# LayerNorm sums from Gram blocks on TensorE, and a parameter stage in one searched order, in a four-layer kernel

## The chip, the cores and the metric

One core of one Trainium2 chip. The metric is the device time of one execution in microseconds (us). Single runs of one kernel here spread by about 0.5% (528 us before: 526.3 to 528.9, with one run at 530.7), so several runs are taken, and each kernel is set against the kernel before on the same chip. The experiments came in three batches, the first and third on one chip and the second on another. Kernels of different batches are therefore compared by their ratios to the kernel before; 11 of the third batch's 12 runs of before are those of the first. Engines: PE (TensorE), DVE (VectorE), ACT (ScalarE), POOL (GpSimd), SP (sync, which issues most transfers). "PEld" in the profile is PE's weight load. The "granted clock" is the PE clock that the chip allowed in a stretch, as a share of full speed (1.00). Every run told of here was classed as fast, not disturbed.

## The reference

Input x is 2048 x 512 in bf16. Four layers, each added to x after a LayerNorm: convolution, attention, convolution, attention. Both convolutions have the same parameters.

```python
def conv(u, A_re, A_im, B_re, B_im, C_re, C_im, log_dt, Dskip):   # u: LayerNorm(x)
    dt = exp(log_dt)[:, None]                     # 512 channels
    P = exp((dt * A)[:, :, None] * l)             # 512 x 128 modes x 2048 steps, l = 0..2047
    K = einsum("dn,dnl,dn->dl", C, P, dt * B).real
    return irfft(rfft(u padded) * rfft(K padded))[:2048] + u * Dskip
def attend(x):                                    # 32 heads of 16, window of 8 at distance 2
    ...                                           # cut
x = x + conv(layernorm(x)); x = x + attend(layernorm(x))
x = x + conv(layernorm(x)); x = x + attend(layernorm(x))
```

## The kernel before

The first stage makes from the parameters the powers of each mode: a *ladder* of ten squarings (lambda, lambda^2, lambda^4, ...), whose values are cast to bf16 *multipliers*. From these DVE builds, for each of eight groups of 64 channels, a *table*: levels 0 to 3 and "high" double the filled part each time (two products and a sum per level), then three products with larger powers. TensorE contracts the table to the convolution kernel. In the same stage the first LayerNorm takes its mean and variance with one DVE statistic instruction per 512 elements of a token, 16 in all.

```python
def ladder(nc, pp, pst, identf, raw, M, cb, fill):
    ...                                             # exp, sin, cos; turned to modes by TensorE
    for i in range(11):
        if i < 10:
            nc.scalar.activation(sq[:], cur[:], ACT.Square)
            nc.vector.scalar_tensor_tensor(nxt[:, 1, :], cur[:, 0, :], 2.0, cur[:, 1, :], ALU.mult, ALU.mult)
            nc.vector.tensor_tensor(nxt[:, 0, :], sq[:, 0, :], sq[:, 1, :], ALU.subtract)
        multipliers(i, cur)                         # up to 4 casts f32 -> bf16, all on ACT
        ...                                         # coefficients at i = 0, the 48th power at i = 5
        fill(i)

def fill(i):
    if 1 <= i <= 4:
        ln.gather(X, 0, (i - 1) * 4, i * 4)         # bn_stats, four at a time
    if i == 4:
        ln.finish(0, NJ)                            # 16 bn_aggr, sqrt, reciprocal, offset
    if i == 10:
        for j in range(NJ):                         # 16 normalisations, all on ACT
            nc.scalar.activation(X[:, j, :], X[:, j, :], ACT.Identity, bias=ln.nb[:, j:j + 1], scale=ln.rstd[:, j:j + 1])
```

The rest of the kernel (first convolution, attention, second convolution, attention) is written as four *plans*: a list of operations with what each must wait for, some of them with alternatives (`either`: on ACT or on DVE, by transfer or by TensorE), and a list of numbers, found by a search, that says in which order they are issued and which alternative is taken.

```python
def run(self):
    order = [int(i) for i in ORDERS[Plan.turn].split()]
    ...
    for i in order:
        fn, after, way = self.ops[i]
        assert done.issuperset(after)
        fn(); done.add(i)
```

## Time and profile before

| | before |
|---|---|
| time, median (3 runs) | 528.13 us (527.34 to 528.93) |
| span of the profile | 525.1 us |
| DVE / PE / ACT busy | 91% / 78% / 65% |
| first stage, 20 to 62 us | DVE and ACT full, PE nearly idle |
| DVE from 62 to 180 us | 116.1 of 118 us busy |

The busy share alone says that DVE is the engine to relieve; the stretches, which the prediction shows below, say where: with DVE full and later stages that wait for it, a microsecond saved early can travel far. It is not certain that it does, because between 20 and 62 us ACT is full as well.

### The profile page before, as it was taken

Reading aid. Unit: us, or ns where it says so; the run is one execution under the profiler, and the core shown is the slowest. Engines: PE = TensorE matmul, PEld = TensorE weight load, DVE = VectorE, ACT = ScalarE, POOL = GpSimd, SP = SyncE. Lnnn points to the kernel's source line nnn. Section 1 sums busy time; section 2 is a strip of 40 time slices with the busy share of each in tenths; the row PEclk is TensorE's granted clock in tenths of the full one; section 3 lists DMA queues with packets and bytes.
Section 4 is the critical chain, followed back from the end, with each engine's and each line's share of the span. In section 5 each row is a group of like instructions: output and inputs, shape, how many; then the busy total and the mean of one; then the engine's idle time right before and its main releaser. Section 6 shows DMA issues by size and latency. Waiting matters only on the chain.

```text
span 525.1 us, 11929 instructions
## 1 busy us (share of the span) xinstructions
PE 407.9 (78%) x4973; PEld 239.1 (46%) x4973; DVE 475.4 (91%) x803; ACT 339.2 (65%) x505; POOL 12.9 (2%) x62
## 2 busy tenths in 40 slices
PE   0201367788869769899999788969997999998896
PEld 0100245456646647543456234555774334653342
DVE  4999999999999999759899998889989597999995
ACT  3999966886866768772766137989996436641230
POOL 0000000000000003100000000000000000000000
PEclk9999997989998999999999999999999999998998
DMA  8300073149125253460011422679401600222252
GB/s 264 156 1 0 0 142 92 46 131 163 43 104 122 48 157 108 138 121 31 0 62 49 103 40 41 182 214 167 82 2 20 101 31 31 71 56 55 41 134 88
DMA packets 88923, 45.10 MB, mean 86 GB/s; under 512 B 74923, under 2 KB 81068, under 8 KB 88612
## 3 DMA queue, kind: packets, MB, share of 16 engines
q1 hardware_dynamic: 87284, 43.93, 34.3%
q8 instruction: 39, 0.64, 0.5%
q10 hardware_dynamic: 1584, 0.39, 0.4%
q14 instruction: 16, 0.13, 0.1%
HBM read 15.77 MB, written 8.13 MB: 46 GB/s over the span
## 4 chain that ended last, share of the span: by engine, by line
DVE 34%; PE 32%; ACT 10%; issue 9%; DMA 4%; SPq 0%; POOL 0%; DVEq 0%; ACTq 0%
PE ps_qk L1193 10%; DVE prod L1356 7%; PE ps_v L1213 4%; PE Lp L1254 3%; DVE Y2tab L545 3%; DVE Ttab L545 3%; DVE Ttab L488 3%; DVE Ttab L481 3%; DVE Ttab L480 3%; DVE ln_st_b L150 3%; PE ps_o L1429 2%; PE po L1372 2%; PE po L1377 1%; ACT X L598 1%; DVE Ttab L497 1%
## 5 line engine op out<-in xcount | busy, mean ns | idle before, releaser
L1244 DVE TENSOR_TENSOR prod<-qT,kT 128x2048 bf16<-128x2048 bf16 (+1 forms) x80 | 77.2, 1007 | 12.3 <-ACT kT L1198 11.7
L1356 DVE TENSOR_TENSOR prod<-VX,L 128x2048 bf16<-128x2048 bf16 (+2 forms) x96 | 77.6, 868 | 1.7 <-PE po L1377 0.9
L1193 PE MATMUL ps_qk<-xnT,wqk 128*128 128x512 bf16 x256 | 62.3, 381 | 0.6 <-DMA xnT<-xn 0.4
L1372 PE MATMUL po<-prod,sb_ident 128*128 128x512 bf16 x224 | 56.1, 388 | 6.9 <-DVE prod L1356 4.5
L1372 PEld LDWEIGHTS <-sb_ident 128*128 128x128 bf16 x224 | 21.8, 99 | 35.4 <-issue 12.0
L1193 PEld LDWEIGHTS <-wqk 128*128 128x128 bf16 x256 | 22.1, 98 | 31.5 <-issue 10.4
L1213 PE MATMUL ps_v<-wv,xnT 128*128 128x256 bf16 x256 | 32.9, 273 | 1.4 <-ACT xnT L1171 1.2
L1392 ACT CAST ot<-po 128x1024 bf16<-128x1024 f32 x14 | 13.6, 1014 | 29.7 <-PE po L1372 29.7
L1254 PE MATMUL Lp<-prod,sb_bones 128*32 128x512 bf16 x256 | 28.7, 388 | 4.2 <-DVE prod L1244 4.2
L520 PE MATMUL ps_sum<-Ttab,sb_ident 128*128 128x512 bf16 x18 | 7.7, 426 | 30.6 <-DVE Ttab L480 27.6
L716 ACT CAST Z<-ps_s 128x1024 bf16<-128x1024 f32 (+1 forms) x32 | 29.5, 996 | 0.2
L558 PE MATMUL psk<-Ttab 128*32 128x64 bf16 x1024 | 21.7, 204 | 9.6 <-DVE Ttab L545 6.0
L1218 ACT CAST VX<-ps_v 128x512 bf16<-128x512 f32 x32 | 18.8, 587 | 15.6 <-PE ps_v L1213 15.6
L545 DVE TENSOR_TENSOR Ttab<-Ttab,MPA 128x2048 bf16<-128x2048 bf16 (+2 forms) x20 | 28.5, 1436 | 0.3
L561 PE MATMUL psk<-Y2tab,Ttab 128*32 128x48 bf16 x1024 | 21.6, 199 | 8.4 <-issue 7.6
L1429 PE MATMUL ps_o<-wo_t,oT 128*128 128x512 bf16 x112 | 28.0, 379 | 0.0
L1213 PEld LDWEIGHTS <-xnT 128*128 128x128 bf16 x256 | 23.2, 98 | 9.6 <-issue 4.6
L545 DVE TENSOR_TENSOR Y2tab<-Ttab,MPB 128x6144 bf16<-128x6144 bf16 (+1 forms) x13 | 27.2, 2123 | 0.0
L1198 ACT CAST qT<-ps_qk 128x512 bf16<-128x512 f32 x24 | 14.0, 584 | 19.1 <-PE ps_qk L1193 19.1
L150 DVE BATCH_NORM_STATS2 ln_st_b<-X 128x6 f32<-128x128 bf16 (+2 forms) x80 | 22.9, 356 | 3.7 <-ACT X L856 3.3
L1198 ACT CAST kT<-ps_qk 128x512 bf16<-128x512 f32 x26 | 15.2, 584 | 15.9 <-PE ps_qk L1193 15.9
L558 PEld LDWEIGHTS <-Ttab 128*32 128x32 bf16 x1024 | 19.6, 102 | 11.9 <-issue 11.1
(220 smaller groups left out, 1030.6 us busy)
## 6 DMA issues: line engine op xcount, KB each, us to landing
X<-in_A_u_dram SPq DMA_DIRECT2D x8, 512.0 KB, 5.4
kt_scratch<-sp_k SPq DMA_DIRECT2D x16, 256.0 KB, 2.8
Kt<-kt_scratch SPq DMA_DIRECT2D x16, 256.0 KB, 5.9
out_dram<-X SPq DMA_DIRECT2D x4, 512.0 KB, 2.7
k_scratch<-KTq SPq DMA_DIRECT2D x7, 256.0 KB, 2.6
KT<-k_scratch SPq DMA_DIRECT2D x7, 256.0 KB, 2.8
VX<-VX SPq DMA_DIRECT2D x4, 448.0 KB, 3.7
kT<-kT SPq DMA_DIRECT2D x8, 192.0 KB, 2.2
```

Of the source, the lines that this page charges most:

```text
L150: self.nc.vector.bn_stats(self.st[:, j, part, :], X[:, j, a:b])
L545: nc.vector.tensor_tensor(d, src.to_broadcast([128, c, n, 2 * EYB]), mm.to_broadcast([128, c * n, EYB, 2]), ALU.mult)
L558: nc.tensor.matmul(o.rearrange("e (s i) -> e s i", s=2), xs, T[:, 1:3, h, m // 2, :, t], start=(m == 0), stop=False, skip_group_check=True)
L716: nc.scalar.copy(box["Z", kind, dc][:, 0:n // 8, :, jq * 32:(jq + 1) * 32].rearrange("p g r k -> p r g k"), box.pop(("s1", kind, dc, jq))[ ...
L1193: nc.tensor.matmul(ps[:], wqk[:, ct, f0:f0 + 128], xnT[:, 4 * s:4 * s + 4, ct, :], start=(ct == 0), stop=(ct == 3))
L1198: copy((qT, kT)[which][fp][:, f2, o:o + 512], box.pop(("qk", which, fp, f2, s))[:])
L1213: nc.tensor.matmul(ps[:, jj].rearrange("p t h d -> p (t h d)"), xnT[:, j + jj, ct, :], wv[:, ct, fp * 256:(fp + 1) * 256], start=(ct == 0) ...
L1244: nc.vector.tensor_tensor(pr[:, 0:n2], qT[fp][:, a:a + n2, j0 * 128:j0 * 128 + 1024], kT[fp][:, a:a + n2, c0:c0 + 1024], ALU.mult)
L1254: nc.tensor.matmul(Lp[r0:r0 + 32, w // 4, :], bones[:, w % 4, :], pr[:, f2 - a, hb * 512:(hb + 1) * 512], start=(n == 1), stop=(n == 4), s ...
L1356: nc.vector.tensor_tensor(p2[:, 0:nj].rearrange("p j t d h -> p (j t) d h"), VX[:, fp, NV + a:NV + a + nj].rearrange("p j (t d h) -> p (j ...
L1372: nc.tensor.matmul(po[:, c:c + 512], ident[:], p2[:, k + j:k + j + 2].rearrange("p j t d h -> p (j t d h)"), start=(n == 1), stop=(n == W))
L1429: nc.tensor.matmul(ps, box["oT"][:, ft // 2, j, ft % 2, :], wo_t[:, ft, :], start=(ft == 0 and not res), stop=(ft == 3))
```

## The change

The intent: take the LayerNorm sums away from DVE, which is full, and give them to PE, which is idle. X is turned by eight DMA transposes. The 32 x 32 Gram blocks of 32 tokens with themselves have the sums of squares on their diagonals; a product with ones gives the sums. DVE then only masks the diagonals and reduces, once for all 2048 tokens. Second, the whole first stage becomes a fifth plan with a searched order and alternatives of its own (casts and normalisations on ACT or DVE), and the first table and the first levels of the second move into it. Third, the parameters are loaded in runs of 1 KB per partition instead of 256 B. All five orders were searched anew, those of the unaltered later layers too.

```diff
-        eng.dma_start(t[:], prm[name].rearrange("(t p) n -> p t n", p=128))
+        eng.dma_start(t[:], prm[name].rearrange("(p t) n -> p t n", p=128))
...
+def prepare(nc, pp, pst, raw, identf, block, ones, M, cb, T, ln, X):
+    pl = Plan(ptq=2, sq=2, lad=3)
...
+        B = pl.either(("mb", i), lambda: [act(a_sign(0)), act(a_sign(1))], lambda: follow(act(a_sign(0)), opposite()),
+                      lambda: follow(ve(v_sign(0)), opposite()))
...
+        def turn(j2=j2):
+            nc.sync.dma_start(xT[:, j2 * 2:j2 * 2 + 2].rearrange("c j t p -> c (j t) p"),
+                              X[:, j2 * 2:j2 * 2 + 2].rearrange("p j c -> p (j c)"), transpose=True)
+        def mm(j2=j2):
+            for j in (j2 * 2, j2 * 2 + 1):
+                for ct in range(4):
+                    nc.tensor.matmul(rows[:, j:j + 1], xT[:, j, ct, :], ones[:, 0:1], start=(ct == 0), stop=(ct == 3), ...)
+                for ct in range(4):
+                    for g in range(4):
+                        x = xT[:, j, ct, g * 32:g * 32 + 32]
+                        nc.tensor.matmul(gram[g * 32:g * 32 + 32, j, :], x, x, start=(ct == 0), stop=(ct == 3), ...)
+    o = vec(0.61, lambda: nc.vector.tensor_tensor(own[:], gram[:], block[:].unsqueeze(1).to_broadcast([128, NJ, 32]), ALU.mult), gs)
+    o = vec(0.61, lambda: nc.vector.tensor_reduce(sq[:], own[:], axis=AX.X, op=ALU.add), o)
...
+    for lev in range(4):                             # first table, half by half
+        for x in (1, 0):
+            a = vec(2 * us, lambda lev=lev, x=x: T.level(0, lev, x, x + 1), o[x], casts[lev if x else lev + 6])
+            o[x] = vec(us, lambda lev=lev, x=x: T.level_sum(0, lev, x, x + 1), a)
...
+    pl.run()
```

## The prediction

> **What bounds the kernel now.** I read the busy shares in 40 slices first, then the busy time by stretches, then the groups of instructions and the order of time in the first 67 us.
>
> The page's slices (one digit is 13.1 us, in tenths of busy time):
>
> ```profile
> PE   0201367788869769899999788969997999998896
> DVE  4999999999999999759899998889989597999995
> ACT  3999966886866768772766137989996436641230
> ```
>
> DVE (VectorE) is at nine tenths from slice 2 to slice 16, so from 13 to about 205 us; that is the stage which the change rewrites (parameters, first LayerNorm, kernel tables, first convolution). ACT is full only in slices 2 to 5, and PE is nearly empty there. The busy time by stretches (stretch, length, then each engine's busy us with its count) says it in numbers:
>
> ```profile
> 9.00:20.00 11.00, 3.52 (x13) 2.38 (x14) 10.97 (x19) 6.30 (x11) 0.00 (x0) 1.00 0.85 339
> 20.00:31.00 11.00, 0.89 (x4) 0.49 (x3) 11.00 (x19) 11.00 (x20) 0.00 (x0) 1.00 0.00 1
> 31.00:42.00 11.00, 0.00 (x0) 0.00 (x0) 11.00 (x38) 10.97 (x19) 0.00 (x0) 1.00 0.00 1
> 42.00:52.00 10.00, 2.15 (x6) 0.73 (x7) 9.86 (x18) 10.00 (x18) 0.00 (x0) 1.00 0.00 0
> 52.00:62.00 10.00, 2.78 (x16) 1.47 (x15) 9.90 (x8) 10.00 (x15) 0.00 (x0) 1.00 0.00 0
> 62.00:70.00 8.00, 5.61 (x261) 4.87 (x260) 7.13 (x6) 6.64 (x9) 0.00 (x0) 1.00 0.49 82
> ```
>
> From 20 to 62 us DVE and ACT (third and fourth busy figure) are both full and PE is idle. From 62 to 180 us DVE is busy 116.13 of 118 us. So a microsecond of DVE work taken out before 62 us, or of DVE idleness filled, should move everything up to about 205 us forward, provided ACT does not hold it back. The groups of the first 64 us show the work in question (busy us, mean ns):
>
> ```profile
> L150 DVE BATCH_NORM_STATS2 ln_st_a<-X 128x6 f32<-128x512 bf16 x16 | 10.3, 683 | 1.9 <-DMA X<-in_A_u_dram 1.9
> L421 DVE TENSOR_TENSOR lad<-sq 128x512 f32<-128x512 f32 x10 | 6.9, 687 | 0.0
> L159 DVE BATCH_NORM_AGGREGATE ln_mv_a<-ln_st_a 128x2 f32<-128x6 f32 x16 | 1.2, 153 | 0.0
> L598 ACT ACTIVATE X<-X,ln_nb_a,ln_rstd_a 128x512 bf16<-128x512 bf16 x16 | 11.4, 799 | 0.0
> L418 ACT ACTIVATE sq<-lad 128x1024 f32<-128x1024 f32 x9 | 9.4, 1047 | 0.0
> ```
>
> And the order of time shows three places where order, not work, costs:
>
> ```profile
> 9.03 1.88 DVE L150 BATCH_NORM_STATS2 ln_st_a<-X 128x6 f32<-128x512 bf16 x3 [1.89 <-DMA X<-in_A_u_dram]
> 10.83 0.67 DVE L367 TENSOR_TENSOR cs<-sh 128x512 f32<-128x512 f32 x1
> ...
> 15.58 1.06 ACT L418 ACTIVATE sq<-LAM 128x1024 f32<-128x1024 f32 x1
> ...
> 50.95 11.37 ACT L598 ACTIVATE X<-X,ln_nb_a,ln_rstd_a 128x512 bf16<-128x512 bf16 x16
> ...
> 64.38 1.23 DVE L480 TENSOR_TENSOR Ttab<-Ttab,MUA 128x2048 bf16<-128x2048 bf16 x1 [0.80 <-ACT Ttab L525]
> ```
>
> DVE stands 1.89 us for the first rows of X although other work is there; three statistics then delay the cosine, so the ladder of squarings starts only at 15.58; and the second table's level 3 waits 0.80 us for a copy on ACT which stood behind the 16 normalisations. My reference point is the end of that pair of level 3 products of the second table: 66.7 us (the next DVE instruction starts at 66.77).
>
> Overlap matters in the counting: a 128x512 f32 tensor operation lasts 0.69 us, but starts follow at 0.60. I count starts: 0.60 per 512 f32, 0.29, 0.33, 0.60, 1.14, 2.2, 3.27 for bf16 products of 256, 512, 1024, 2048, 4096, 6144; 0.60 per 512-element statistic; on ACT 0.52 per cast, 0.95 per square, 0.71 per normalisation.
>
> **What the Trainium skill says.** "VectorE: DVE Perf Modes", perf-mode tier table: a tensor_tensor in f32, and tensor_reduce in any type, have only the 1x mode; bf16 tensor_tensor 2x; tensor_scalar and copy up to 4x. The trace agrees where it has the case: 687 ns for 512 f32 elements and 684 for 1024 bf16. So the new product with the block mask and the reduction should each cost the 0.60 of an f32 operation. "ScalarE: Activation LUTs", what ACT_TABLE_LOAD costs: about 1283 ns; the trace has three of 1.28 here, and the change needs the same three functions. "TensorE: Matmul & The Clock Gate", back-to-back issue gap: about 25 ns is the floor for up to 64 columns. The trace is faster where four column groups alternate: the table contraction of before issues about 120 such small matmuls per us (15 pairs of four and four in 1.0 us). The 256 Gram matmuls (32x32 outputs in four column groups) are then some 2 to 6 us of an idle PE. "DMA: Bandwidth & Descriptors", DMA Transpose (X-bar): 2-byte types into SBUF, which this is; before's 32 such transposes land a median of 3.5 us after issue and cost about 1.3 us of issue each.
>
> **The change, part by part (DVE before the reference point).** Before: 4.38 to 66.74 is 62.4 us, with idle 0.64 (parameter load), 1.89 and 0.80; so 59.0 us of work.
> - Removed: 16 statistics x 0.60 = 9.6 and 16 aggregations, 1.1: -10.7.
> - Added for the statistics: mask product 0.61, reduction 0.61, three 16-wide operations of about 0.12: +1.6.
> - The first table is now built half by half (levels 0 to 3, twice the instructions at half the size): six operations of about 0.25 / 0.29 / 0.33 / 0.60 instead of three of 0.29 / 0.33 / 0.60 / 1.14: +0.6 +0.75 +0.2 +0.2 = +1.75.
> - Choices that I read by counting the operations in the order in which the new plan makes them and looking up which numbers its order holds: eight multiplier casts go from ACT to DVE (one full cast 0.6, seven half-size bf16 copies at 0.33), +2.9; three of 16 normalisations at 0.32, +1.0; one evacuation of the turned parameters, +0.6; the second table's level 2 sum on DVE instead of PE and ACT, +0.6.
> Sum: -10.7 + 8.4 = -2.3, so 56.7 us of DVE work. The large statistic saving is thus mostly spent on relieving ACT.
>
> ACT, same way: from the start of the ladder it had 62.3 - 15.6 = 46.7 us without a gap. New: 10 squares 9.5, 38 casts (46 before) 19.8, two coefficient copies 1.0, table load with root 1.6, 13 normalisations 9.2: 41.1 us, starting when the ladder can start. With the statistics out of the way and the parameters contiguous (1 KB runs instead of 256 B), I put that at about 13 us, so ACT ends near 54 to 56, and DVE still has the 2.2 + 3.3 us of products after ACT's last multiplier. DVE stays the bound: start near 4.1, 56.7 of work, 0.5 to 2 of idleness for loads and the start of the ladder: 61.3 to 62.8, say 62.0. Gain at the reference point: 4.7 us.
>
> After it, the convolution's own choices, counted the same way: DVE loses two joins and two level sums, gains two other sums and three evacuations: +1.0 us by the durations of those shapes; ACT and PE lose three PE-made turns of spectra (2.8 and 1.4 us), which become DMA. As DVE is 98% busy there, I give back 1.0 of the gain and take 0.3 for less waiting. The convolution should end about 4.0 us earlier. The two attention layers and the second convolution keep their operations; about a dozen choices move (in the first attention layer two residual additions go from DVE to PE and ACT, -0.9 us of DVE; in the last, two evacuations). I credit the new orders with 1.0 us in all. That is my judgement, not a count. Sum: 528.1 - 4.0 - 1.0 = 523.1.
>
> **Rivals.** (a) The statistics fully pay: all 9.1 us (10.7 less 1.6) come through because ACT is what really paces 20 to 62 us, and the moves to DVE fill holes. For it: ACT has no gap there. Against: DVE has none either, and 8 of those 9 us are visibly spent on it. It would give 517 to 519. (b) The turned copy of X comes late and takes the place of the statistics: the eight transposes wait for X on the sync queue and for each other. X landed from 9 us; eight times 1.3 from about 11 plus 3.5 ends near 25; the mask product stands in DVE's order after about 26 us of work, near 30. Margin 4 us; if it fails, DVE or the normalisations wait and the time is 525 to 528. The 2 MB of transform constants are now issued after these transposes, near 23 us, and needed only near 50. (c) What is gained early is lost at the convolution's end: after 207 us before, DVE waits for PE and ACT (1.03 and 1.93 us in single waits), a chain of transfers, turns and copies. If that chain sets the end, only half arrives: about 526. Against: its start hangs on the last table, which DVE makes.
>
> **Range.** The count of DVE work is good to about 1.5 us, its idleness to 1, the later orders to 2. Together about 3: 519.5 to 526.3. Faster by over 2% needs below 517.8, which only rival (a) reaches: 0.07. Slower by over 2%: 0.01.
>
> **What would show it.** Right: none of the 16 first statistics; the mask product and reduction at about 0.69 us with no wait before them; the first square near 13 us; DVE busy about 57 us before the second table's level 3 products end, and that end near 62; normalisations over by 54; the first contraction about 4 us earlier than 65.3; the stretch from there to the last layers unchanged in length to 1 us. Wrong: a DVE wait for PE's Gram sums, half-size copies of multipliers that cost 0.6 instead of 0.33 (then 2 us less gain), or a gain after 205 us larger than before it.

## The result

The changed kernel takes 519.89 us (median of 4 runs, 519.01 to 520.22), before in the same rounds 527.74 (527.29 to 528.93). The ratio is 0.9845, 95% interval 0.9824 to 0.9867. A ratio is formed from the fast runs of both kernels and is near the ratio of their means (here 519.75 over 527.92), not quite that of the medians; for the experiments it is given as recorded, and the listed runs give it again to about 0.001. The saving is 7.85 us; the prediction said 523.1, a saving of 5.0, with 519.5 as the low end of its range. So it holds, but near its edge.

Where the time went, from the two profiles (us from the start; the profiled runs differ by 6.7 us):

| point | before | changed | shift |
|---|---|---|---|
| DVE through with the work of the first stage (first table, second table to the level 3 products) | 66.7 | 60.4 | -6.3 |
| first contraction on PE | 65.3 | 61.5 | -3.9 |
| last table products start on DVE | 193.6 | 187.7 | -5.9 |
| last X of the first convolution arrives (statistics start) | 219.5 | 216.4 | -3.2 |
| first projection of the first attention | 228.3 | 225.0 | -3.3 |
| first matmul of the second convolution | 344.1 | 340.8 | -3.3 |
| last matmul of the second convolution | 396.9 | 392.1 | -4.8 |
| end | 525.1 | 518.4 | -6.7 |

Three things stand in this table: a gain of 6.3 us in the first stage, a loss of 2.7 between 188 and 220 us, and another 3.4 us gained after 340 us, where the operations are the same but for a few choices of engine. (The medians differ by 7.85 us, the two profiled runs by 6.7; the table cannot place the other 1.1.)

A caution: the granted clock and small waits move such points. The changed kernel, profiled again with the experiments, had a span of 520.3. A single profile's points are good to 1 or 2 us, stage lengths in undisturbed stretches to some tenths.

The page of the changed kernel, busy tenths in 40 slices (13.0 us each):

```profile
PE   1600768688869887899999879979997999997896
DVE  6999999999999998768899998799899498999995
ACT  4999877569658756653655437989996447632330
```

PE now has six tenths of work in slice 2 (mostly the Gram blocks), where it had two; the first runs of full slices end one slice earlier, for DVE after slice 15 instead of 16 and for ACT after slice 4 instead of 5. The stretches of the same time as shown of before (stretch, length, then busy us and count of PE, PEld, DVE, ACT, POOL, then clock, DMA share and GB/s):

```profile
9.00:20.00 11.00, 6.96 (x136) 5.24 (x136) 10.31 (x23) 6.08 (x10) 0.00 (x0) 1.00 0.80 199
20.00:31.00 11.00, 4.47 (x200) 3.75 (x200) 10.66 (x23) 11.00 (x20) 0.24 (x2) 1.00 1.08 196
31.00:42.00 11.00, 0.00 (x0) 0.10 (x1) 10.80 (x31) 10.97 (x18) 0.00 (x0) 1.00 0.31 126
42.00:52.00 10.00, 0.37 (x2) 0.21 (x2) 10.00 (x16) 10.00 (x17) 0.00 (x0) 1.00 0.00 0
52.00:60.40 8.40, 6.23 (x37) 4.18 (x37) 8.40 (x5) 8.20 (x12) 0.00 (x0) 1.00 0.01 2
```

Both engines are full, to the end of the stage. The change has not made one of them idle; it has made both finish together and earlier. The groups that replaced the statistics (busy us, mean ns, idle before):

```profile
L657 DVE TENSOR_TENSOR own<-gram,sb_block 128x512 f32<-128x512 f32 x1 | 0.7, 679 | 0.0
L658 DVE TENSOR_REDUCE sqs<-own 128x16 f32<-128x512 f32 x1 | 0.7, 679 | 0.0
```

Two instructions (and three small ones of 0.16 us) stand for 32, and DVE waits for neither. The order of time of the changed kernel's start and of its casts:

```profile
3.89 0.69 DVE L490 TENSOR_TENSOR tb<-raw_A_im,dtw 128x512 f32<-128x512 bf16 x1
...
5.98 0.69 DVE L490 TENSOR_TENSOR t<-raw_C_im,raw_B_re 128x512 f32<-128x512 bf16 x1 [0.94 <-DMA raw_C_im<-in_A_C_im_dram]
...
7.31 0.63 ACT L513 ACTIVATE sh<-rnd 128x512 f32<-128x512 f32 x1 [0.78 <-DVE rnd L490]
...
14.26 1.06 ACT L595 ACTIVATE sq<-LAM 128x1024 f32<-128x1024 f32 x1
...
20.72 0.29 DVE L575 TENSOR_SCALAR MUB<-MUB 128x512 bf16<-128x512 bf16 x1
20.92 0.68 DVE L603 SCALAR_TENSOR_TENSOR lad<-lad 128x512 f32<-128x512 f32 x1
```

The ladder's first square starts at 14.26 instead of 15.58 us, and a bf16 copy that replaces an ACT cast costs DVE 0.20 us from start to start.

The first stage's gain closes as a sum. Before, DVE's share of this work ran from 4.38 to 66.74 with 3.33 us of waits: 59.0 us of work. Changed, it runs from 3.69 to 60.40 with 1.7 us of waits (0.94 for C_im, 0.3, 0.3 and 0.2 for ACT): 55.0 us. Less work 4.0, less waiting 1.6, earlier start 0.7: 6.3 us.

### The profile page after: what moved, and what is told of

The parts are those of the page before. It is cut to its first block, busy times and chain, and to the rows that moved or that the text cites. A ratio compares the mean times of both kernels' runs of the same rounds, so it can differ in the third digit from the quotient of the medians.

```text
span 518.4 us, 12520 instructions
## 1 busy us (share of the span) xinstructions
PE 415.7 (80%) x5250; PEld 245.0 (47%) x5267; DVE 471.6 (91%) x802; ACT 330.0 (64%) x488; POOL 13.0 (3%) x63
## 4 chain that ended last, share of the span: by engine, by line
DVE 39%; PE 29%; ACT 9%; issue 8%; DMA 2%; SPq 0%; DVEq 0%; ACTq 0%
PE ps_qk L1319 10%; DVE prod L1482 7%; DVE Y2tab L454 4%; DVE ln_st_b L153 4%; DVE Ttab L454 3%; PE Lp L1380 3%; PE ps_v L1339 3%; DVE prod L1370 2%; DVE Ttab L390 2%; DVE Ttab L397 2%; DMA VX<-VX 2%; DVE Ttab L389 2%; DVE Ttab L405 1%; DVE pb L928 1%; DVE Ttab L406 1%
## 5 line engine op out<-in xcount | busy, mean ns | idle before, releaser
L1498 PE MATMUL po<-prod,sb_ident 128*128 128x512 bf16 x213 | 54.8, 379 | 6.7 <-DVE prod L1482 4.5
L836 PE MATMUL ps_s<-X,sb_F 128*128 128x128 bf16 x128 | 10.9, 241 | 26.7 <-ACT X L667 23.6
L836 PEld LDWEIGHTS <-sb_F 128*128 128x128 bf16 x256 | 16.1, 103 | 31.3 <-issue 25.6
L1324 ACT CAST kT<-ps_qk 128x512 bf16<-128x512 f32 x29 | 16.9, 585 | 19.6 <-PE ps_qk L1319 19.5
L454 DVE TENSOR_TENSOR Ttab<-Ttab,MPA 128x2048 bf16<-128x2048 bf16 (+2 forms) x20 | 28.4, 1434 | 0.7 <-ACT Ttab L434 0.5
L955 ACT CAST VT<-vp 128x512 bf16<-128x512 f32 x31 | 16.9, 593 | 13.4 <-PE vp L951 12.0
```

Source lines behind the costliest of these rows:

```text
L454: nc.vector.tensor_tensor(d, src.to_broadcast([128, c, n, 2 * EYB]), mm.to_broadcast([128, c * n, EYB, 2]), ALU.mult)
L836: nc.tensor.matmul(o, F1[:, j, r, :], rhs(j), start=True, stop=not dk)
L1498: nc.tensor.matmul(po[:, c:c + 512], ident[:], p2[:, k + j:k + j + 2].rearrange("p j t d h -> p (j t d h)"), start=(n == 1), stop=(n == W))
```

## The experiments

All gave correct results. Each was run in five rounds. "Changed" is 519.9 us (ratio 0.9845) unless said otherwise. Orders are lists of operation numbers; moving a number moves the operation in its engine's instruction order, and all waits are made anew from the data.

### Statistics back on DVE

```diff
         def turn(j2=j2):
-            nc.sync.dma_start(xT[...], X[...], transpose=True)
+            pass
         def mm(j2=j2):
-            ...                                   # 8 row sums and 32 Gram matmuls
+            ln.gather(X, 0, j2 * 2, j2 * 2 + 2)
-    o = vec(0.61, lambda: nc.vector.tensor_tensor(own[:], gram[:], block...), gs)
-    o = vec(0.61, lambda: nc.vector.tensor_reduce(sq[:], own[:], axis=AX.X, op=ALU.add), o)
+    o = vec(0.61, lambda: None, gs)
+    o = vec(1.1, lambda: ln.gathered(0, NJ), o)
```

(Cut: the three small operations on the Gram sums, emptied, and the offset taken from the aggregates again.)

> The changed kernel, with the first LayerNorm's statistics back as 16 statistics and 16 aggregations on DVE (at the places where the Gram matmuls stood in the order), no turned copy of X, no Gram matmuls, no mask product and reduction; everything else as changed. My theory: the stage is bound by DVE, so the 10.7 - 1.6 = 9.1 us of DVE work come back nearly whole; the DVE work before the reference point ends near 69 instead of 60.4 us, and the time is 527 to 529 us, no better than before. Rival (ACT paces this stage, DVE has slack): at most 4 us come back, 520 to 524 us.

Measured 528.03 us (527.43 to 531.42), ratio 1.0022 (0.9996 to 1.0049): 9.3 us more than the changed kernel by the ratios (1.77% of 528), 8.1 by the medians. The large product that ends the stage starts at 65.59 instead of 57.05 us. From 20 to 60 us the two engines stand so:

```profile
20.00:60.00 40.00, 0.37 (x2) 0.21 (x2) 39.76 (x97) 32.82 (x52) 0.00 (x0) 1.00 0.00 0
```

DVE 39.76 of 40, ACT 32.82 (in the changed kernel 39.46 and 39.77). The rival is refuted for this order: with the statistics on DVE it is DVE that paces, and of the 9.1 us counted for them 8.5 come back at the end of the stage.

### The eight casts back on ACT

```diff
-ORDERS[0]: ... 54 ... 55 ... 68 ... 69 ... 62 ... 63 ... 84 ... 85 ... 132 ... 133 ... 176 ... 177 ... 208 ... 209 ...
+ORDERS[0]: ... 50 ... 51 ... 66 ... 67 ... 60 ... 61 ... 82 ... 83 ... 130 ... 131 ... 174 ... 175 ... 206 ... 207 ...
```

> The changed kernel, with the eight multiplier casts that it makes on DVE (one full, seven half-size copies) back on ACT as full casts, at the same places of the order. DVE loses about 0.6 + 7 x 0.2 = 2.0 us of work, ACT gains 8 x 0.52 = 4.2. If DVE alone set the end of the stage it would gain up to 2 us (518 us). My theory: the two engines are balanced to within 2 us, ACT's last cast and the two products after it then set the end, so that it loses 1 to 3 us: 521 to 523 us.

Measured 525.0 us (524.24 to 526.43), ratio 0.9951 (0.9933 to 0.9968): 5 us lost, more than the 1 to 3 expected. DVE now waits where it did not (who waited for whom, total us, times, longest):

```profile
DVE lad L607 <- ACT sq L595: 3.4, 5, 1.2
DVE Ttab L365 <- ACT cb L540: 0.6, 1, 0.6
```

ACT is busy 39.89 of the 40 us from 20 to 60, DVE 36.37. So with Gram sums and without the moved casts ACT paces the stage: the large product at its end starts at 60.16, 3.1 us later than changed. The rest of the loss, about 2 us, lies behind the stage. In its profile the first attention was 1.4 us longer (117.2 us), and the traces show with what: in five of the 14 profiles (this one, short runs, two groups moved, the second profile of four groups moved, last two orders) that stage took 116.7 to 117.2 us, and in each of these the granted clock of PE falls for 4 to 8 us, some 80 us into the stage; in the nine others it stays at full speed there and the stage took 115.8 or 115.9. The two profiles of one and the same kernel, with four groups moved, at this place (stretch, length, busy figures as above, clock):

```profile
301.50:305.50 4.00, 3.59 (x22) 1.91 (x24) 4.00 (x5) 1.40 (x2) 0.32 (x3) 1.00 0.64 120
303.60:307.60 4.00, 3.65 (x16) 1.88 (x17) 4.00 (x5) 1.34 (x2) 0.00 (x0) 0.57 0.64 120
```

So this microsecond goes with the clock of the single execution, not with the order or the edit. The two experiments together show what the change is: with the 9 us taken from DVE and all casts left on ACT, ACT sets the pace, and by the ratios only 2.6 us of the saving are left (0.9951). The casts that went to DVE are worth most of the rest. What the first table in halves and the three normalisations on DVE are worth was not run by itself.

### Both back

> The changed kernel with both undone: statistics on DVE as in the run with the statistics put back, and the eight casts on ACT as in the run with the casts put back. What is left of the rewritten stage is its order, the contiguous parameter load, the first table in halves and three normalisations on DVE. My theory: DVE has 2 us less work than with the statistics alone put back, and ACT has slack there because DVE paces, so this is 1 to 2 us faster than that run: 526 to 528 us, about the time of before less the gain of the later orders. Rival (the searched order of the stage is worth several us without the Gram sums): 521 to 524 us.

The edit is the two above together. Measured 528.54 us (527.02 to 529.48), ratio 1.0013 (0.9986 to 1.0039), not distinguishable from the run with the statistics alone put back (1.0022). The 1 to 2 us expected for it did not appear: from 20 to 60 us DVE was busy 38.76 and ACT 35.28, each waiting a little for the other in an order that was searched for another balance. The rival, that this searched order by itself is worth several us, is refuted: without Gram sums and casts nothing of the gain is left. The stages say it more sharply. The second table's level 3 products are over at 66.7 us before, but DVE is through with the first stage's work only at 68.6 here, and the projections start at 231.8 instead of 228.3; the 3.4 us that the later orders gain then make up for it. Whether an order searched anew for the old operations would do better was not run.

### Parameters in short runs

```diff
-    for name, eng in (("A_im", nc.scalar), ("A_re", nc.sync), ...):
-        eng.dma_start(t[:], prm[name].rearrange("(p t) n -> p t n", p=128))
+    for name, eng in (("A_im", nc.sync), ("A_re", nc.scalar), ...):
+        eng.dma_start(t[:], prm[name].rearrange("(t p) n -> p t n", p=128))
```

(log_dt and the two copies that put the turned parameters into channel order are put back too.)

> The changed kernel, with the parameters loaded as before (runs of 256 B, log_dt in runs of 2 B, A_im on the sync queue and A_re on the ACT queue, parameters kept in the old column order). In the traces the first DVE instruction starts at 3.69 us with the contiguous load and at 4.38 before, and with the contiguous load DVE still waits 0.94 us for C_im. My theory: all of the stage starts 0.7 us later and the wait for C_im grows by about 1: 521 to 522 us. Rival (other engines or the order hide the start): 520 us.

Measured 522.34 us (520.90 to 523.82), ratio 0.9893 (0.9868 to 0.9918): 2.5 us lost by the ratios, with intervals of 0.25% that leave 1 to 4. DVE's waits at the start were

```profile
DVE dtw L508 <- ACT dtb L506: 4.4, 1, 4.4
DVE t L490 <- DMA raw_C_im<-in_A_C_im_dram: 1.0, 1, 1.0
DVE tb L490 <- DMA raw_A_im<-in_A_A_im_dram: 0.7, 1, 0.7
```

against 3.7, 0.9 and none in the changed kernel: 1.5 us, and the stage's last large product starts 1.6 us later (58.61). The contiguous load is worth about that. The rest is not explained: in the profile 1.0 us of it is the first attention with the clock's fall told of above (116.8 us), and the low mean clock of this profile (0.935) is no reason by itself, since the changed kernel's fastest run (519.01 us) had 0.941.

### The later orders alone

The first run has the changed kernel with the three last orders (attention, convolution, attention) of before, the second the kernel before with those three of the changed one.

> The changed kernel, with the orders of the last three plans (attention, convolution, attention) put back to those of before. Changed kernel 519.9 us, before 527.7. In the trace of the changed kernel the start of the first attention's projections is 3.3 us earlier than before, the end of the second convolution 4.8, the end of the program 6.7. My theory: the first 3.3 us come from the rewritten stage and the other 3.4 from the newly searched later orders; so this run should take 523.0 to 523.8 us, with the projections starting near 225.0 and the second convolution from its first spectrum matmul to its last taking the 52.2 us of before, not 50.7. Rival: the later gains come with the shifted start (which transfers meet which work, the granted clock), not with the orders; then it stays near 520 us.

Measured 523.36 us (521.68 to 525.48), ratio 0.992 (0.9898 to 0.9941): 3.5 us more than changed, as expected. The projections start at 225.3, the second convolution takes 52.9 us (before 52.8, changed 51.3), the last attention 127.5 (128.2 and 126.3).

> The kernel before, with only the three later orders of the changed kernel. My theory: it gains what the first run loses, some 3.4 us, of it about 0 in the first attention, 1.5 in the second convolution, 1.8 in the last attention: 524 to 525 us. Rival (gain comes with the shifted start): 527 to 528 us.

Measured 526.74 us (525.43 to 527.44), ratio 0.9978 (0.9961 to 0.9995): 1.2 us gained, less than the 3.4 expected. Its second convolution is 51.2 and its last attention 126.6 us, so those gains are there. But its first attention starts 2.6 us late, at 230.9 instead of 228.3. At the end of the first convolution DVE stands so before its statistics (total, times, longest):

```profile
DVE ln_st_b L150 <- ACT X L856: 5.3, 3, 3.9
```

One wait of 3.9 us, where before had 1.9 at this place. The lists give the reason. The old end of the convolution finishes the quarters of X in the order 2, 1, 0, 3 and the old attention asks for them so; the new pair has 3, 2, 0, 1. Mixed, the attention asks first for the quarter that comes last. The orders of neighbouring plans belong together, though not every mixture is costly: the opposite one, in the first run above, delayed the projections by only 0.3 us.

> The kernel before, with only the orders of the second convolution and of the last attention taken from the changed kernel; the first attention keeps its own. The run with all three gained only 1.2 us; in its trace the first attention's projections start 2.6 us later than before, because DVE first waits 3.9 us for a quarter of X that the old end of the convolution finishes last, while the other two stages are 1.5 and 1.6 us shorter. My theory: without that mismatch the two orders gain about 3 us: 524.3 to 525.5 us. Rival (the later gains need the earlier start): 526.5 us or more.

Measured 526.19 us (524.93 to 527.48), ratio 0.9969 (0.9949 to 0.9989): 1.6 us, not 3. In its profile the late start is mostly gone (228.9), the second convolution took 52.2 and the last attention 126.9 us, but the first attention, unaltered, took 117.1 us instead of 115.8. This is one of the five profiles with the clock's fall there (0.72 and 0.85 in two stretches of 4 us), so its longer first attention needs no mixture to explain it. What can be said of the second convolution: in the eleven other profiles with its new order it took 51.1 to 51.6 us, and in all of these the first attention too had its new order; with both old it took 52.8 and 52.9. The new order after the old attention, this run, took 52.2. So 1.2 to 1.8 us belong to the pair of orders, and one profile shows about 0.6 for the convolution's alone.

### The end of the first convolution

In the profile of the changed kernel eight statistics of the second LayerNorm stand on the chain of waits shortly after the last table product; the chain from 182 us on has them in its pieces (start, us, what):

```profile
186.59 1.81 DVE Y2tab L454 x3
...
190.87 2.62 DVE ln_st_b L153 x8
```

They could be computed any time before 217 us, and DVE waits 2.3 us at 205 us. Moving them costs no new wait.

```diff
-ORDERS[1]: ... 398 589 602 396 600 ... 571 611 572 569 ...
+ORDERS[1]: ... 589 602 600 ... 571 611 572 398 396 569 ...
```

> The changed kernel, with eight 256-wide statistics of the second LayerNorm (2.6 us of DVE work, standing at 190.8 us in front of the last spectrum products) moved behind the eight 128-wide statistics at 203.0 us, just before the 2.3 us wait of DVE for X. In the trace the last table product ends 5.9 us earlier than before, but the first attention's projections only 3.3: my theory is that the difference of 2.6 us was lost at the end of the convolution, where the searched order puts these statistics on the path. Then this run gains 1 to 2.5 us: 517.4 to 519 us. Rival: the end of the convolution is set by the PE and ACT chain of the last kernel piece, and nothing changes (520 us).

Measured 519.3 us (518.62 to 519.97), ratio 0.9837 (0.9813 to 0.9861). By the time alone it is not distinguishable from the changed kernel (0.9845). The trace shows what was asked for: DVE's waits from 188 to 220 us, before the move

```profile
DVE ln_st_b L153 <- ACT X L981: 4.3, 2, 2.3
DVE VT L955 <- PE vp L951: 1.0, 1, 1.0
DVE pa L927 <- ACT sp_k L1041: 0.6, 1, 0.6
```

are 2.9 us in all after it, and the projections start at 222.6 instead of 225.0. The first attention then took 116.7 instead of 115.8 us, again with the clock's fall in it, so the time shows less than the projections.

```diff
-ORDERS[1]: ... 397 587 ... 395 605 ... 653 648 655 650 657 658 ...
+ORDERS[1]: ... 587 ... 605 ... 653 397 648 655 650 657 395 658 ...
```

(on top of the two above)

> As the run with two groups moved, and two more groups of four 256-wide statistics (1.3 us each) moved into the two later waits of DVE in the convolution's end (1.03 us for PE, 1.93 us for ACT). My theory: a further 0.5 to 1.5 us, 516.5 to 518.5 us, if the products of the last piece are what PE waits for. Rival: the moved statistics delay the last evacuation by as much as they free, and it is no better than with two moved, or 1 us worse.

Measured 518.34 us (517.23 to 520.05), ratio 0.9822 (0.9796 to 0.9848). Projections from 221.5 us. The waits for X are shorter and that for PE is gone, but a new one stands before them, for ACT's copy of a kernel spectrum:

```profile
DVE pa L927 <- ACT sp_k L863: 2.2, 1, 2.2
DVE ln_st_b L153 <- ACT X L981: 0.9, 2, 0.6
```

It was repeated beside the changed kernel itself:

> The changed kernel unaltered, so that it stands in the same rounds as the next two: 519 to 520.5 us.

> The kernel with four groups of statistics moved, again, beside the changed kernel on the same chip: 1.3 to 2.5 us faster than it in the same rounds (its first measurement was 518.3 us, in other rounds than the changed kernel's 519.9; the span of its profile was 3.0 us shorter).

In those rounds the changed kernel took 520.04 us (519.68 to 522.04, ratio 0.9852) and the kernel with four groups moved 518.32 (517.19 to 520.41, ratio 0.9826). The difference of 1.7 us by medians is within what was expected; the two intervals (0.9831 to 0.9873 and 0.9805 to 0.9848) overlap a little, so 1 to 2 us is likely, not proven to the tenth. In both profiles of it the waits for X and for PE are down to 0.9 us, with 2.2 and 3.4 us of the new wait, and the projections started at 221.5 and 223.6, against 225.0 and 226.6 in the two profiles of the changed kernel. Part of that is an earlier start of this end. From the start of the last table products to the projections it is 37.3 us in both profiles of the changed kernel (34.7 before), 34.2 with two groups moved, 34.3 and 35.5 with four, and 35.8 in the next experiment, where they stay moved. The granted clock of this stretch was 1.00 in the three profiles of these two kernels but 0.95 in the changed kernel's two and in the next experiment's, so 1.5 us are shown at equal clock, by one profile, and how much of the rest is the clock's was not separated. So a good part of what the convolution's end had lost was a matter of which work stands where. The rival, a PE and ACT chain that cannot be moved, is refuted for that part; the new wait for ACT shows that such a chain comes next, and that groups three and four add anything is not shown.

### No wait for C_im

```diff
-ORDERS[0]: ... 7 5 8 25 9 21 10 20 24 22 ...
+ORDERS[0]: ... 7 5 8 9 10 20 25 21 24 22 ...
```

(on top of the four groups moved)

> The kernel with four groups of statistics moved, with three operations of the parameter stage exchanged on DVE: the subtraction that gives the reduced phase comes before the products of C and B, and the product that needs only C_re and B_re before those that need C_im. In the changed kernel DVE waits 0.94 us for C_im and ACT then 0.78 us for the subtraction. My theory: most of the 0.94 us goes, and the stage moves forward by 0.6 to 0.9 us: 0.4 to 0.9 us faster than the kernel with the four groups moved, in the same rounds. Rival: the start of the ladder or ACT takes the time up, no difference.

Measured 517.77 us (515.94 to 518.59), ratio 0.9806 (0.9783 to 0.9829). Against the four moved groups (0.9826) that is about 1 us by the ratios and 0.55 by the medians, as expected, but the intervals overlap widely, so the time alone doesn't show it. The trace does show the mechanism at the start of the stage:

```profile
5.69 0.68 DVE L490 TENSOR_TENSOR t<-raw_C_re,raw_B_re 128x512 f32<-128x512 bf16 x1
6.29 0.69 DVE L490 TENSOR_TENSOR t<-raw_C_im,raw_B_re 128x512 f32<-128x512 bf16 x1
```

No wait stands before the product with C_im any more, the sine starts at 6.55 instead of 7.31 us, and the first square at 13.35 instead of 14.26. Against the changed kernel in the same rounds neither the intervals (upper end 0.9829, lower end 0.9831) nor the single runs (slowest 518.59, fastest 519.68) overlap: this version beats both kernels, 9.9 us below before and 2.3 below the changed one.

## Why the prediction was right, and where its sizes were off

**The bound.** Right. With the statistics put back on DVE, 8.5 of their 9.1 us come back, and DVE is busy 39.76 of 40 us. (This is shown for the changed kernel; before, both engines were full, and no run takes work from ACT alone there.) Rival (a), that ACT was the real pace setter and DVE's 9 us come through whole, is wrong in that form: with the Gram sums and the casts left on ACT, ACT does set the pace, and the moved casts are the price of the saving.

**The sum of the first stage.** Its mechanism held, with three terms off, all in the same direction, so that 4.7 us of gain became 6.3. The work on DVE came out at 55.0 us instead of 56.7. The half-size copies follow each other at 0.20 us, not 0.33 (seven of them, 0.9 us); the full cast is a tensor_scalar that lasts 0.42 us, and a tensor_scalar of that length is followed after 0.33, where I had used the 0.60 of a tensor_tensor; and the operations of the first table's halves follow at about 0.18 (128 elements) and 0.20 (256) instead of the 0.25 and 0.29 assumed. The 256-element figure came from rows of level 0, where the same size is slower in the changed trace too (0.29 at level 0, 0.20 at level 1); that was the error. The start came at 3.69 us instead of "near 4.1". Idleness, 1.7 us, lay within the 0.5 to 2 given.

**ACT.** The counted end "near 54 to 56" was met: its last cast ends at 55.7, normalisations at 54.1. The first square was put at 13 and came at 14.26.

**Gram sums.** Rival (b) did not happen, but with less margin than said. The transposes begin at 12.66 us and are issued for 11.49 us; the last lands only near 27.4, not 25, the last Gram matmuls end near 28.4, and the mask product stands at 29.49. The margin is 1.1 us, not 4. PE needs 0.43 us for the four row sums and 16 Gram matmuls of one 128-token block, 6.9 us in all; the Gram matmuls alone show 0.30 us for a block, 4.8 in all, within the 2 to 6 us given for them. (The 120 small matmuls per us of the prediction hold near 69.4 us of the contraction before; in its first us there were 89.)

**The convolution.** Predicted: of 4.7 us, 1.0 given back by the choices and 0.3 regained, 4.0 left. Measured: of 6.3 us, 3.2 left. Between the end of the first stage and the last statistics DVE took 155.9 us instead of 152.8; its busy time rose by 0.7 (147.9 against 147.2), near the 1.0 counted. Its waits rose from 4.3 to 6.9 us, where I had expected fewer. Rival (c), loss at the convolution's end, is therefore partly what happened, but for another reason than the one I gave: in good part not a fixed chain on PE and ACT, but statistics placed in front of work that PE was waiting for. Moving them brought the projections forward by 2.4 to 3.5 us in the profiles, of which 1.5 are shown at equal clock. The step that failed here is "take 0.3 for less waiting", and with it the sign given for being right, that the stretch from the reference point to the last layers keeps its length to 1 us: to the second convolution it grew by 3.0 us (277.4 to 280.4).

**The later layers.** The other step that failed is "I credit the new orders with 1.0 us in all". Putting the old ones back cost 3.5 us. By stages, 1.5 us is the second convolution's and 1 to 2 the last attention's; the first attention gained nothing (115.8 us in both). I had counted which choices move and found them few; but the order of the same operations is not visible in such a count. Put alone into the kernel before, the same orders gained only 1.2 to 1.6 us, of which the mismatch of the quarters explains one case; in the other, 1.3 us of the profile go with the clock's fall, and whether the runs without a profile had it too is not on record. The prediction's sign of being wrong, a gain after 205 us larger than before it, was nearly met: 5.9 us stood at the last table products, but 3.2 at the last X, with 3.5 more after that.

The total fell inside the range by luck in part, because three misjudgements partly cancel: the stage +1.6, the convolution's end -2.4, the later orders +2.4.

## What to carry to other kernels

When two engines are full in the same stretch, taking work from one of them gains only a part (here 2.6 of 8 us) until work of the other can cross over: count both, and provide alternatives that can cross over. Do not judge a searched order by the operations it chooses; compare stage by stage, and check the orders of neighbouring stages together, because one asks for its data in the sequence in which the other delivers it. Before a longer stage is put down to an order, look at the granted clock in that stage: here a fall of a few us went with about 1 us in five of 14 profiles. Where a large early gain shrinks later, look at the chain of waits for work that could be done at any time and stands in front of work that cannot wait.

## What the Trainium skill lacked or had wrong

- "ScalarE: Activation LUTs", what ACT_TABLE_LOAD costs, says that a switch of tables costs the load of about 1283 ns and about 1380 ns of drain, 2.66 us in all. Here the load was 1.28 us, and the next activation follows at once: in the last experiment the load starts at 5.26 us and the sine at 6.55; before the root it starts at 35.75 in the changed kernel and the root at 37.05. A switch cost 1.30 us; no drain shows.
- "VectorE: DVE Perf Modes", perf-mode tier table, gives durations at 2048 elements and has no row for the statistics instruction. The runs show 683 ns for 512 bf16 elements (as slow as an f32 tensor_tensor), and that what counts in a full queue is the distance of starts: 0.60 us for operations of 0.69, 0.20 us for bf16 single-source copies of 512 elements that last 0.29.
- "TensorE: Matmul & The Clock Gate", back-to-back issue gap, has a floor of about 25 ns for up to 64 columns, without mention there of column groups; the page treats them elsewhere, in its part on packing small matmuls. Matmuls into four column groups in turn were issued at about 8 to 11 ns each in the contraction (126 matmuls in its first us in the changed kernel, 89 before); a block of 16 Gram matmuls and four row sums took 0.43 us.
